# V loaded like q and k and turned on TensorE, and chosen rows fetched by a gathering DMA, in a fused attention and routing kernel

## The chip, the cores and the metric

The kernel runs on one core of one Trainium2 chip, as one launch. The metric is the time of one execution on the device in microseconds. Before the change three runs gave 177.98 us as median, 177.62 the lowest and 179.37 the highest.

## The reference: what is computed

Two stages follow each other. The first is attention in chunks: 4 batches, 8 heads, 768 positions, 64 values per head. Each chunk of 32 queries sees 8 memory rows and the context from 16 positions before the chunk to 8 after it.

```
for c in range(nc):                       # 24 chunks of 32 queries
    k_full = concat(mem_k, k[l_start:r_end])      # 8 memory rows + up to 56 keys
    v_full = concat(mem_v, v[l_start:r_end])
    a = softmax(q_c @ k_full.T / sqrt(64))
    out[c] = a @ v_full
```

The second stage works on the result x (4 x 768 x 512). A gate picks 128 of the 768 rows in each batch, and only these go through two matrix products.

```
scores = x @ w_gate
top_idx = the 128 rows with the highest score
ye = relu(x[top_idx] @ w1) @ w2           # 512 -> 1024 -> 512
out[top_idx] = x[top_idx] + sigmoid(scores[top_idx]) * ye
```

## The kernel before, in words

The unit of work is a *pair*: heads h and h+4 of one batch side by side on the 128 partitions. There are 16 pairs, n = 4b + pr, four to a batch. The queries and keys of a pair fall into 8 groups of 96 queries. All orders are written out by hand: each engine runs its instructions in program order, and a semaphore wait of one holds up everything behind it on that engine.

**Loads.** q and k come through POOL's queue, cast to fp16 on the way, as rows of 8 positions x 64 values (512 fp32, 2 KB) on 96 partitions (`load_qk`, L79). V comes through the queues of SP and ACT uncast (`load_v`, L83), as rows of two keys (128 fp32, 512 B), with keys on partitions: for each group 60 partitions of key pairs and 4 of memory pairs, in each half of the partitions one head. Neighbouring groups share keys, so each group's 120 keys are read again: 60 x 8 rows per head. All loads of a batch are issued together, two batches ahead.

**A pair.** `tr_q` and `tr_k` turn q and k with 16 small transposes each into one PSUM tile `p_t`, of which there is one; ACT copies q out (L219), DVE copies k out in two instructions (L228), POOL adds the memory keys (L235). `cast_v` copies V's pairs to fp16 (L243 on ACT, L245 on DVE). `scores(n, half)` does 16 matmuls with 64 rows and 64 columns of the array (L261) and three exponentials on ACT (L266). `values(n, half)` does 24 matmuls with 64 rows of the array each, accumulating the even and the odd keys (L287); the two heads use the upper and the lower 64 rows. `normalise` divides by the row sums once per pair on DVE (L294, L295).

**The order.** Iteration n of the main loop (L497) runs scores(n+1, 0), tr_k(n+2), values(n, 0), cast_v(n+2), scores(n+1, 1), tr_q(n+3), values(n, 1), normalise(n). In six gaps per iteration (`hook`) a step of the second stage of the batch before is put in: dot products with the gate vector on DVE (`m_dot`), a transpose that spreads the scores over a row (`m_row`, L345), casts of x to fp16 on ACT (`m_x16`, L339), comparisons of all scores on DVE (`m_cmp`, L369), counts by matmul (`m_count`, L379), selection matrices (`m_select`, L398), the gather of the chosen rows by 24 matmuls with these matrices (`m_gather`, L406), index and gate by six matmuls more (`m_aux`, L416), and the two products (`m_ffn1` L431, `m_ffn2` L440). The result times the gate (L443) is added to the output by an indirect DMA (L444). The last batch's second stage follows the loop (L534 on).

Of the kernel before, what the change touches and what calls it, by code (L numbers as in the profile page):

```python
# [26 lines left out]
def kernel(  # L27
# [55 lines left out]
    def load_v(b, p0, n, engines=(nc.sync, nc.scalar)):  # L83


        t = vbufs[b % 2].rearrange("p n g d -> p (n g) d")
        u = NG * p0
        for hh in range(2):
            h = 4 * hh + p0
            lo = 1 if (b, h) == (0, 0) else 0  # L90
            hi = NG * n - 1 if (b, h + n) == (B - 1, H) else NG * n
            o = 64 * hh
            base = (b * H + h) * HD - 16 * D
            engines[hh].dma_start(out=t[o:o + 60, u + lo:u + hi, :],
                                  in_=_dap(v, base + 96 * D * lo, [[2 * D, 60], [96 * D, hi - lo], [1, 128]]))
            if lo:
                engines[hh].dma_start(out=t[o + 8:o + 60, u, :], in_=_dap(v, base + 16 * D, [[2 * D, 52], [1, 128]]))
            if hi < NG * n:
                engines[hh].dma_start(out=t[o:o + 56, u + hi, :],  # L99
                                      in_=_dap(v, base + 96 * D * hi, [[2 * D, 56], [1, 128]]))  # L100
        for hh in range(2):
            for i in range(n):
                nc.sync.dma_start(out=t[64 * hh + 60:64 * hh + 64, u + NG * i:u + NG * (i + 1), :],
                                  in_=_dap(mem_v, (b * H + 4 * hh + p0 + i) * n_mem * D,
                                           [[2 * D, 4], [0, NG], [1, 128]]))
# [481 lines left out]
```

## Time and profile before

| | before |
|---|---|
| median of 3 runs | 177.98 us |
| the profiled execution: device time | 178.1 us |
| its span, first to last instruction | 176.3 us |
| mean granted TensorE clock | 0.873 |
| PE (matmuls) busy | 118.3 us, 67% |
| DVE busy | 88.5 us, 50% |
| ACT busy | 82.8 us, 47% |
| POOL busy | 28.5 us, 16% |
| bytes read from HBM, written | 25.49 MB, 7.34 MB |

Busy times are sums over the span; the stages have different limits, so they are read stage by stage. The 1.8 us between span and device time lie around the first and last instruction. The first pair's iteration starts at 25.0 us, the fifth's (batch 1) at 56.5, the ninth's at 94.3, the thirteenth's at 123.9; the loop ends at 152.0.

### The profile page before, as it was taken

The page shows a single profiled execution, that of the slowest core. Times are in us where ns is not written, and L with a number is a line of the kernel's source. Part 1 is how long each engine was busy: PE and PEld are TensorE (multiplying, and loading weights), DVE is VectorE, ACT ScalarE, POOL GpSimd, SP SyncE. Part 2 cuts the span into 40 slices and gives each one's busy share as a digit, 9 for nine tenths or more (in the row PEclk, how much of TensorE's full clock was granted, in tenths as well). Part 3 has the DMA queues.
Part 4 walks back from the last instruction along what each step waited for, and adds up shares of the span by engine and source line. Part 5 has one row for each costly group of instructions (what it writes and reads, how often), then busy time and mean ns, then how long its engine had stood idle before and what let it go on. Part 6 is the DMA issues. An engine that isn't in the chain of part 4 may idle for free.

```text
span 176.3 us, 5308 instructions
## 1 busy us (share of the span) xinstructions
PE 118.3 (67%) x2280; PEld 95.9 (54%) x2280; DVE 88.5 (50%) x275; ACT 82.8 (47%) x163; POOL 28.5 (16%) x57
## 2 busy tenths in 40 slices
PE   0005379996019999798198875999878687456820
PEld 0005367885018878687165565887656576245700
DVE  2303403650035978854025979733897592775010
ACT  0001399650076879431554796447779046030300
POOL 7805900500000113000003300000500000200030
PEclk9999999999999999999858997569995559965795
DMA  5999999999999898999920465000159000059104
GB/s 127 215 223 205 229 216 226 231 227 218 209 194 269 217 116 156 290 264 181 189 60 5 63 200 161 6 0 4 13 128 279 10 0 4 0 77 294 51 0 59
DMA packets 29211, 24.75 MB, mean 140 GB/s; under 512 B 1423, under 2 KB 24963, under 8 KB 29187
## 3 DMA queue, kind: packets, MB, share of 16 engines
q0 software_dynamic: 9136, 9.47, 34.0%
q1 hardware_dynamic: 12271, 11.01, 24.4%
q10 hardware_dynamic: 7780, 3.93, 9.9%
q8 instruction: 18, 0.29, 0.7%
q14 instruction: 6, 0.05, 0.1%
HBM read 25.49 MB, written 7.34 MB: 186 GB/s over the span
## 4 chain that ended last, share of the span: by engine, by line
DMA 31%; PE 28%; DVE 18%; ACT 7%; issue 7%; ACTq 4%; POOLq 1%; SPq 0%; DVEq 0%
DMA v<-in_v_dram 19%; PE p_x L287 8%; DMA v<-in_mem_v_dram 6%; DVE gr L369 6%; PE p_t L211 5%; DVE junk L332 5%; PE p_m L440 4%; DMA out_dram<-x 4%; PE p_s L261 4%; PE p_m L431 3%; ACTq L99 3%; PE p_m L406 3%; ACT es L266 3%; DMA out_dram<-y,idx 3%; DVE x L295 2%
## 5 line engine op out<-in xcount | busy, mean ns | idle before, releaser
L266 ACT ACTIVATE es<-p_s,maskb 128x256 f16<-128x256 f32 x96 | 38.9, 489 | 26.1 <-PE p_s L261 20.4
L287 PE MATMUL p_x<-vc,es 64*96 64x65 f16 (+1 forms) x768 | 31.8, 235 | 0.7 <-DVE x L295 0.7
L287 PEld LDWEIGHTS <-es 64*96 64x96 f16 (+1 forms) x768 | 25.3, 136 | 5.3 <-issue 0.6
L228 DVE COPY kw<-p_t 128x480 f16<-128x480 f16 x32 | 19.5, 650 | 13.7 <-PE p_t L211 13.7
L261 PE MATMUL p_s<-qT,kw 64*64 64x96 f16 x512 | 23.7, 255 | 0.5 <-ACT es L266 0.5
L444 POOL DMA_INDIRECT out_dram<-y,idx x4 | 6.8, 1700 | 95.1 <-PE p_t L211 54.2
L261 PEld LDWEIGHTS <-kw 64*64 64x64 f16 x512 | 18.5, 143 | 4.6 <-issue 2.2
L211 PE MATMUL p_t<-ident,k 96*64 96x96 f16 x256 | 11.7, 254 | 11.8 <-ACT qT L219 11.8
L243 ACT CAST vc<-v 128x768 f16<-128x768 f32 x16 | 13.8, 861 | 10.8 <-DMA v<-in_mem_v_dram 10.8
L211 PEld LDWEIGHTS <-k 96*64 96x64 f16 x256 | 9.4, 143 | 13.2 <-issue 12.2
L332 DVE SCALAR_TENSOR_TENSOR junk<-x,wgb 128x512 f32<-128x512 f32 (+2 forms) x30 | 16.0, 579 | 0.1
L295 DVE TENSOR_TENSOR x<-p_x,rd 128x768 f32<-128x768 f32 x16 | 15.3, 957 | 0.6
L211 PE MATMUL p_t<-ident,q 96*64 96x96 f16 x256 | 12.3, 263 | 3.8 <-DVE kw L228 3.8
L219 ACT COPY qT<-p_t 128x768 f16<-128x768 f16 x16 | 13.1, 817 | 3.4 <-PE p_t L211 3.4
L294 DVE RECIPROCAL rd<-p_x 128x12 f32<-128x12 f32 x16 | 3.7, 228 | 21.8 <-PE p_x L287 21.8
L369 DVE TENSOR_SCALAR gr<-brow,scr 128x768 f16<-128x768 f32 x24 | 13.3, 614 | 0.1
L211 PEld LDWEIGHTS <-q 96*64 96x64 f16 x256 | 10.1, 149 | 5.3 <-issue 4.2
L245 DVE TENSOR_SCALAR vc<-v,ones 128x128 f16<-128x128 f32 x32 | 7.6, 290 | 10.4 <-DMA v<-in_mem_v_dram 10.0
L339 ACT CAST x<-x 128x1024 f16<-128x1024 f32 (+2 forms) x11 | 12.6, 1148 | 0.0
L431 PEld LDWEIGHTS <-w_sb 128*128 128x128 f16 x128 | 8.7, 108 | 6.4 <-issue 4.4
L379 PEld LDWEIGHTS <-gr 128*128 128x128 f16 x144 | 5.4, 104 | 10.3 <-DVE gr L369 10.0
L431 PE MATMUL p_m<-xeT,w_sb 128*128 128x128 f16 x96 | 7.2, 236 | 5.5 <-ACT hT L433 4.5
(90 smaller groups left out, 115.5 us busy)
## 6 DMA issues: line engine op xcount, KB each, us to landing
out_dram<-x SPq DMA_DIRECT2D x4, 1152.0 KB
v<-in_v_dram SPq DMA_DIRECT2D x3, 960.0 KB
q<-in_q_dram POOLq DMA_DIRECT2D x6, 384.0 KB, 12.3
k<-in_k_dram POOLq DMA_DIRECT2D x6, 384.0 KB, 14.9
w_sb<-in_moe_w_dram POOLq DMA_DIRECT2D x2, 1024.0 KB, 24.2
v<-in_v_dram ACTq DMA_DIRECT2D x2, 960.0 KB
out_dram<-x SPq DMA_DIRECT2D x4, 384.0 KB
v<-in_v_dram ACTq DMA_DIRECT2D x1, 930.0 KB
```

The costliest lines, as they stand in the source:

```text
L211: nc.tensor.transpose(out=p_t[64 * h:64 * h + 64, j, 2:98], in_=src[b][:, pr + 4 * h, 64 * j:64 * j + 64], identity=ident16[0:96, 0:96])
L219: nc.scalar.copy(out=qT, in_=p_t[:, :, 2:98].rearrange("p j t -> p t j"))
L228: nc.vector.tensor_copy(out=kw[:, :, s, 0:60].rearrange("p g (t j) -> p g t j", j=4), in_=_sap(p_t, 100 * s, [[12, NG], [1, 15], [200, 4]]))
L243: nc.scalar.copy(out=vc[:, 1:7, :, 0:64], in_=vt[:, pr, 1:7, :].rearrange("p g (s d) -> p g s d", d=D))
L261: nc.tensor.matmul(out=p_s[o:o + 64, s, 96 * gi:96 * gi + 96], lhsT=kw[o:o + 64, g, s, :], rhs=qf[o:o + 64, 96 * g:96 * g + 96], start=Tru ...
L266: nc.scalar.activation(out=es[:, :, :, 32 * c:32 * c + 32], in_=pv[:, :, :, 32 * c:32 * c + 32], func=AF.Exp, bias=maskb[:, c:c + 1], scal ...
L287: nc.tensor.matmul(out=p_x[r0:r1, h, c0:c0 + 65], lhsT=es[o:o + 64, s, gi, q0:q1], rhs=vc[o:o + 64, GROUPS[half][gi], s, :], start=(s == 0 ...
L295: nc.vector.tensor_tensor(out=xs[b].rearrange("p g (h n d) -> p n h g d", n=NP, d=D)[:, pr], in0=pv[:, :, :, 0:64], in1=rd.to_broadcast([1 ...
L332: nc.vector.scalar_tensor_tensor(out=o, in0=i, scalar=1.0, in1=w, op0=ALU.mult, op1=ALU.mult, accum_out=dst[:, bl:bl + 1])
L339: nc.scalar.copy(out=o, in_=i)
L369: nc.vector.tensor_scalar(out=m.gr[:, bl, :], in0=m.brow, scalar1=m.scr[:, bl:bl + 1], scalar2=None, op0=ALU.is_lt)
L431: nc.tensor.matmul(out=p_h[:, 0, 128 * fi:128 * fi + 128], lhsT=w1_sb[:, dch, f0:f0 + 128], rhs=m.xeT[:, dch, :], start=(dch == 0), stop=( ...
```

## The change

V is loaded exactly like q and k, through POOL's queue, as 2 KB rows cast to fp16. It is turned by 16 transposes into `p_t` (`tr_v`), copied by ACT into groups of 128 keys with 15 + 1 columns (15 of the sequence, one memory row) per eight, and turned back by eight 128 x 128 transposes per pair (`back_v`), so that all 128 keys of a group lie on the partitions. k gets the same column layout. Scores then need 8 matmuls per half (64 rows, 128 columns of the array) in place of 16, values 12 with all 128 rows in place of 24, and each half is normalised by itself. k's copy out of `p_t` becomes one DVE instruction of 1024 elements with unit step, and so is the copy of V's back-transposes. An iteration has eight hooks in place of six, and the second stage's steps are spread over them. For batches 0 to 2 the chosen rows are fetched from the output in HBM by an indirect DMA with 128 indices (`m_fetch`), transposed in fp32 (`m_rows`), and their gate is computed from them (`m_gate1`); the casts of x, the gather by matmul and the two-part gate remain for the last batch only. The gated result is written by ACT in place of DVE. Indirect DMAs name the output only up to the batch in question.

```diff
+    pvv = ctx.enter_context(tc.tile_pool(name="pvv", bufs=1, space=bass.MemoryType.PSUM))
...
-    def load_v(b, p0, n, engines=(nc.sync, nc.scalar)):
...
+    def load(b, src, dst, h0, n, step=1):
         nc.gpsimd.dma_start(out=dst[:, h0:h0 + step * (n - 1) + 1:step, :],
                             in_=_dap(src, (b * H + h0) * HD, [[512, 96], [step * HD, n], [1, 512]]))
...
+    def load_batch(b):
+        for h0 in (0, 4):
+            load(b, k, k16s[b], h0, 4)
+            load(b, v, v16s[b], h0, 4)
+            load(b, q, q16s[b], h0, 4)
...
+    for src, dst in ((mem_k, memk16), (mem_v, memv16)):
+        nc.gpsimd.dma_start(out=dst, in_=_dap(src, 0, [[D, n_mem], [n_mem * D, B * H], [1, D]]))
+    load(0, v, v16s[0], 0, 2, 4)
     for pr in range(1, NP):
-        load_qk(0, k, k16s[0], pr, 2, 4)
-        load_qk(0, q, q16s[0], pr, 2, 4)
+        load(0, k, k16s[0], pr, 2, 4)
+        load(0, q, q16s[0], pr, 2, 4)
+        load(0, v, v16s[0], pr, 2, 4)
...
+    def mem_cols(t, src, n):
+        nc.gpsimd.tensor_copy(out=t.rearrange("p g (j t) -> p g j t", t=16)[:, :, :, 15],
+                              in_=src[:, n:n + 1, :].to_broadcast([128, NG, n_mem]))
     def tr_k(n):
...
-        for s in range(2):
-            nc.vector.tensor_copy(out=kw[:, :, s, 0:60].rearrange("p g (t j) -> p g t j", j=4),
-                                  in_=_sap(p_t, 100 * s, [[12, NG], [1, 15], [200, 4]]))
+        nc.vector.tensor_copy(out=kw.rearrange("p g (j t) -> p g j t", t=16),
+                              in_=_sap(p_t, 0, [[12, NG], [100, 8], [1, 16]]))
+        mem_cols(kw, memkT, n)
+    def tr_v(n):
...
+        transposes(v16s, n)
+        vw = vws[n % SLOTS]
+        nc.scalar.copy(out=vw.rearrange("p g (j t) -> p g j t", t=16),
+                       in_=_sap(p_t, 0, [[12, NG], [100, 8], [1, 16]]))
+        mem_cols(vw, memvT, n)
-    def cast_v(n):
...
+    def back_v(n):
...
+        p_v = pvv.tile([128, NG, 2, D], F16, tag="pv", name="p_v")
+        for g in range(NG):
+            nc.tensor.transpose(out=p_v[:, g, :, :], in_=vws[n % SLOTS][:, g, :], identity=ident16)
+        nc.vector.tensor_copy(out=vcs[n % SLOTS][:, :, :, 0:64], in_=p_v)
...
-            for s in range(2):
-                for h in range(2):
-                    o = 64 * h
-                    nc.tensor.matmul(out=p_s[o:o + 64, s, 96 * gi:96 * gi + 96], lhsT=kw[o:o + 64, g, s, :],
+            for h in range(2):
+                o = 64 * h
+                nc.tensor.matmul(out=p_s[:, h, 96 * gi:96 * gi + 96], lhsT=kw[o:o + 64, g, :],
+                                 rhs=qf[o:o + 64, 96 * g:96 * g + 96], start=True, stop=True)
...
+        p_x = pxx.tile([128, 3, 2, 65], FP, tag="px", name="p_x")
...
+                for h in range(2):
+                    nc.tensor.matmul(out=p_x[r0:r1, i, h, :], lhsT=es[:, h, gi, q0:q1],
+                                     rhs=vc[:, GROUPS[half][gi], h, 0:65], start=True, stop=True)
+        rd = att.tile([128, 3, 2, 1], FP, tag="rd", name="rd")
+        nc.vector.reciprocal(out=rd, in_=p_x[:, :, :, 64:65])
...
+    def m_fetch(b):
...
+        for bl in range(NB):
+            nc.tensor.matmul(out=p_a[:, 0, 0:1], lhsT=m.sel[:, bl, :], rhs=auxs[0][:, bl, 0:1],
+                             start=(bl == 0), stop=(bl == NB - 1))
+        m.idx = mod.tile([128, 1], I32, tag="idx", name="idx")
+        nc.vector.tensor_scalar(out=m.idx, in0=p_a[:, 0, 0:1], scalar1=float(b * S), scalar2=None, op0=ALU.add)
+        m.xe = mod.tile([128, Dm], FP, tag="xe", name="xe")
+        nc.gpsimd.indirect_dma_start(out=m.xe[:, :], out_offset=None, in_=outf[0:(b + 1) * S, :],
+                                     in_offset=bass.IndirectOffsetOnAxis(ap=m.idx[:, :1], axis=0))
+    def m_rows(b):
...
+        for dch in range(4):
+            nc.tensor.transpose(out=p_e[:, 0, 128 * dch:128 * dch + 128], in_=m.xe[:, 128 * dch:128 * dch + 128],
+                                identity=ident)
+        nc.scalar.copy(out=m.xeT.rearrange("p c t -> p (c t)"), in_=p_e[:, 0, :])
+    def m_gate1(b):
...
+        nc.vector.scalar_tensor_tensor(out=junk, in0=m.xe, scalar=1.0, in1=wgb, op0=ALU.mult, op1=ALU.mult,
+                                       accum_out=se)
+        nc.scalar.activation(out=m.gate, in_=se, func=AF.Exp, scale=-1.0)
+        nc.vector.tensor_scalar(out=m.gate, in0=m.gate, scalar1=1.0, scalar2=None, op0=ALU.add)
+        nc.vector.reciprocal(out=m.gate, in_=m.gate)
...
-        nc.vector.tensor_scalar(out=y, in0=p_y[:, 0, :], scalar1=m.gate[:, 0:1], scalar2=None, op0=ALU.mult)
-        nc.gpsimd.indirect_dma_start(out=outf, out_offset=bass.IndirectOffsetOnAxis(ap=m.idx[:, :1], axis=0),
+        nc.scalar.activation(out=y, in_=p_y[:, 0, :], func=AF.Copy, scale=m.gate[:, 0:1])
+        nc.gpsimd.indirect_dma_start(out=outf[0:(b + 1) * S, :], out_offset=bass.IndirectOffsetOnAxis(ap=m.idx[:, :1], axis=0),
...
+        st = {i: [lambda i=i: m_dot(b, (i,))] for i in range(NB)}
+        st[0].insert(0, lambda: m_alloc(b))
+        st[6] = [lambda: m_row(b, 0, 4)]
+        st[8] = [lambda: m_row(b, 4, 6)]
+        for i in range(NB):
+            st[9 + i] = [lambda i=i: m_cmp(b, (i,))]
+        st[14].append(lambda: m_count(b, range(0, 3)))
+        st[15] = [lambda: m_count(b, range(3, 6)), lambda: m_mask(b)]
+        st[17] = [lambda: m_select(b)]
+        st[19] = [lambda: m_fetch(b)]
+        st[24] = [lambda: m_rows(b), lambda: m_gate1(b)]
+        st[26] = [lambda: m_ffn1(b, 0)]
+        st[28] = [lambda: m_ffn1(b, 1)]
+        st[30] = [lambda: m_ffn2(b)]
...
+    mem_rows(memk16, memkT)
     tr_k(0)
-    mem_k(0)
     tr_q(0)
+    mem_rows(memv16, memvT)
+    tr_v(0)
+    scores(0, 0)
     tr_k(1)
+    back_v(0)
+    scores(0, 1)
     tr_q(1)
+    tr_v(1)
     tr_q(2)
     alloc_batch(1)
+    load_batch(1)
...
         scores(n + 1, 0)
         hook(0)
         tr_k(n + 2)
         hook(1)
         values(n, 0)
         hook(2)
+        tr_v(n + 2)
+        hook(3)
         scores(n + 1, 1)
+        hook(4)
+        back_v(n + 1)
+        hook(5)
+        values(n, 1)
+        hook(6)
         tr_q(n + 3)
+        hook(7)
         if pr == 2 and b + 2 < B:
             alloc_batch(b + 2)
+            load_batch(b + 2)
```

## Rows read from the trace of the kernel before

**Rows 1.** The page's span in 40 equal slices: mean busy share of the DMA engines, tenths.
```profile
DMA  5999999999999898999920465000159000059104
```

**Rows 2.** The chain that ended last: start us, length us, what.
```profile
24.67 24.56 DMA v<-in_v_dram
...
79.74 5.86 ACTq L99
...
153.10 4.46 DMA out_dram<-y,idx
```

**Rows 3.** Timeline of PE, first half: start us, us, operation, count, idle before.
```profile
13.89 1.02 PE L170 MATMUL p_mk<-ident,memk 8*64 8x8 f16 x32 [13.89 <-DMA memk<-in_mem_k_dram]
...
24.99 0.85 PE L261 MATMUL p_s<-qT,kw 64*64 64x96 f16 x16 [0.53 <-ACT es L266]
...
34.64 0.85 PE L211 MATMUL p_t<-ident,q 96*64 96x96 f16 x16
35.42 1.13 PE L287 MATMUL p_x<-vc,es 64*96 64x65 f16 x24
36.48 0.85 PE L261 MATMUL p_s<-qT,kw 64*64 64x96 f16 x16
37.26 0.85 PE L211 MATMUL p_t<-ident,k 96*64 96x96 f16 x16
...
52.07 0.85 PE L211 MATMUL p_t<-ident,k 96*64 96x96 f16 x16 [9.50 <-ACT qT L219]
...
61.77 1.11 PE L345 MATMUL p_m<-ident,scr 128*128 128x128 f32 x4
...
87.38 1.86 PE L431 MATMUL p_m<-xeT,w_sb 128*128 128x128 f16 x16 [4.46 <-ACT hT L433]
```

**Rows 4.** DMA queues in two stretches of 4 us, 48:52 and 84:88: packets, MB, share.
```profile
q0 software_dynamic: 750, 0.74, 110.9%
...
q10 hardware_dynamic: 1326, 0.68, 101.2%
```

**Rows 5.** Windows of L211 (transposes): PE busy (count), PEld busy (count), granted clock, DMA, GB/s.
```profile
52.00:56.00 4.00, 1.70 (x32) 1.32 (x31) 1.00 1.10 247
...
88.00:92.00 4.00, 0.85 (x16) 0.66 (x16) 0.50 0.35 69
```

**Rows 6.** Timeline of PE, second half.
```profile
102.76 0.53 PE L211 MATMUL p_t<-ident,q 96*64 96x96 f16 x16
103.22 0.75 PE L287 MATMUL p_x<-vc,es 64*96 64x65 f16 x24
103.90 0.53 PE L261 MATMUL p_s<-qT,kw 64*64 64x96 f16 x16
...
113.24 2.74 PE L406 MATMUL p_m<-sel,x 128*128 128x128 f16 x24
...
117.73 1.12 PE L431 MATMUL p_m<-xeT,w_sb 128*128 128x128 f16 x16
```

**Rows 7.** Groups by line and form: count, busy us, mean ns, idle before.
```profile
L228 DVE COPY kw<-p_t 128x480 f16<-128x480 f16 x32 | 19.5, 650 | 13.7 <-PE p_t L211 13.7
L295 DVE TENSOR_TENSOR x<-p_x,rd 128x768 f32<-128x768 f32 x16 | 15.3, 957 | 0.6
L369 DVE TENSOR_SCALAR gr<-brow,scr 128x768 f16<-128x768 f32 x24 | 13.3, 614 | 0.1
L219 ACT COPY qT<-p_t 128x768 f16<-128x768 f16 x16 | 13.1, 817 | 3.4 <-PE p_t L211 3.4
L245 DVE TENSOR_SCALAR vc<-v,ones 128x128 f16<-128x128 f32 x32 | 7.6, 290 | 10.4 <-DMA v<-in_mem_v_dram 10.0 <-issue 0.4
L294 DVE RECIPROCAL rd<-p_x 128x12 f32<-128x12 f32 x16 | 3.7, 228 | 21.8 <-PE p_x L287 21.8
L443 DVE TENSOR_SCALAR y<-p_m,gate 128x512 f32<-128x512 f32 x3 | 2.3, 751 | 3.3 <-PE p_m L440 3.3
```

**Rows 8.** Waits: engine, line, waited for: us in total, times, longest us.
```profile
PE p_m L379 <- DVE gr L369: 6.0, 10, 1.4
```

More of the change, by code (lines that the diff above doesn't have):

```diff
@@ L67 @@
     ctx.enter_context(tc.manual_schedule())
-    q16s, k16s = {}, {}
-    vbufs = [cst.tile([128, NP, NG, 128], FP, tag=f"v32_{i}", name=f"v32_{i}") for i in range(2)]
+    q16s, k16s, v16s = {}, {}, {}
     def alloc_batch(b):
@@ L77, in alloc_batch @@
         k16s[b] = ld.tile([96, H, 512], F16, tag="k16", name=f"k16_{b}")
-    def load_qk(b, src, dst, h0, n, step=1):
+        v16s[b] = ld.tile([96, H, 512], F16, tag="v16", name=f"v16_{b}")
+    def load(b, src, dst, h0, n, step=1):
         nc.gpsimd.dma_start(out=dst[:, h0:h0 + step * (n - 1) + 1:step, :],
                             in_=_dap(src, (b * H + h0) * HD, [[512, 96], [step * HD, n], [1, 512]]))
-    def load_v(b, p0, n, engines=(nc.sync, nc.scalar)):
[L86 to L105, printed above, removed]
+    def load_batch(b):
[3 more added lines that the diff above has]
+            load(b, q, q16s[b], h0, 4)
     alloc_batch(0)
-    load_qk(0, k, k16s[0], 0, 2, 4)
-    load_qk(0, q, q16s[0], 0, 2, 4)
+    memk16 = cst.tile([n_mem, B * H, D], F16, tag="memk16")
+    memv16 = cst.tile([n_mem, B * H, D], F16, tag="memv16")
+    load(0, k, k16s[0], 0, 2, 4)
+    load(0, q, q16s[0], 0, 2, 4)
     ident16 = cst.tile([128, 128], F16, tag="ident16")
@@ L169, in mem_keys @@
             for hh in range(2):
-                nc.tensor.transpose(out=p_mk[64 * hh:64 * hh + 64, pr, :], in_=memk16[:, b * H + 4 * hh + i, :],
+                nc.tensor.transpose(out=p_mk[64 * hh:64 * hh + 64, pr, :], in_=src[:, b * H + 4 * hh + i, :],
                                     identity=ident16[0:n_mem, 0:n_mem])
-        nc.vector.tensor_copy(out=memkT, in_=p_mk.rearrange("p n (j s) -> p n s j", s=2))
+        nc.vector.tensor_copy(out=dst, in_=p_mk)
     ident = cst.tile([128, 128], FP, tag="ident")
@@ L498 @@
         b, pr = divmod(n, NP)
-        steps = moe_steps(b - 1) if b >= 1 else [[] for _ in range(24)]
+        steps = moe_steps(b - 1) if b >= 1 else {}
         def hook(i):
-            for f in steps[6 * pr + i]:
+            for f in steps.get(8 * pr + i, ()):
                 f()
@@ L509 @@
         tr_k(n + 2)
-        mem_k(n + 2)
         hook(1)
         values(n, 0)
-        cast_v(n + 2)
         hook(2)
+        tr_v(n + 2)
+        hook(3)
         scores(n + 1, 1)
-        hook(3)
+        hook(4)
[3 more added lines that the diff above has]
+        hook(6)
         tr_q(n + 3)
-        hook(4)
-        values(n, 1)
-        normalise(n)
-        hook(5)
+        hook(7)
         if pr == 2 and b + 2 < B:
             alloc_batch(b + 2)
-            for h0 in (0, 4):
-                load_qk(b + 2, q, q16s[b + 2], h0, 4)
-                load_qk(b + 2, k, k16s[b + 2], h0, 4)
-            load_v(b + 2, 0, NP)
+            load_batch(b + 2)
         if n == NPR - 2:
```

116 lines of the change are left out of this document (30 added, 86 removed).

## The prediction

> **What bounds the kernel now.** I read the page's 40 slices first: the DMA engines are nearly full from 0.5 us to about 60 and again from 66 to 90 [rows 1], so the first half may be waiting for data. Then the chain of waits: two of its pieces are transfers or queues of V, 24.56 us for batch 1's rows and 5.86 us in which ACT's queue is held at the issue of batch 3's V (L99) [rows 2]. What they cost is read from PE's timeline, not from their length: PE stands 9.50 us before 52.07 and 4.46 us before 87.38 [rows 3], 14.0 us together. Apart from these two gaps PE sets the pace of the first half alone: from start to start 16 transposes take 0.78 us, a half of values 1.06, a half of scores 0.78 [rows 3], and a pair has two of each: 5.24 us with no gap. In the second half PE is not alone: a pair needs 2 x (0.46 + 0.68) us plus two scores of about 0.46, 3.2 us [rows 6], but batch 2 takes 29.6 us (94.3 to 123.9); DVE's comparisons alone keep PE's counts waiting 6.0 us in all [rows 8].
>
> The two sets of durations are TensorE's two clock levels. At 52 to 56 us the granted clock reads 1.00, yet 32 transposes are 1.70 us busy, exactly the 0.85 per 16 of 88 to 92 us, where it reads 0.50 [rows 5]; at 102.76 us 16 take 0.53 [rows 6]. So durations decide, and the whole first half runs at 1.2 GHz, with PE without a gap from 52 to 76 us. In this trace 2.4 GHz comes only behind the gather's or the FFN's 128 x 128 matmuls: the gather starts at 113.24 and runs at 0.11 us a matmul, the FFN matmuls at 117.73 take 1.12 us where the same 16 took 1.86 at 87.38 [rows 3, 6].
>
> **The change part by part**, against the profiled execution's 178.1 us (span 176.3 plus 1.8 outside). That is 0.1 from the median of 177.98, so no correction is needed. A measurement of this kernel can tell about 1% from no change.
>
> *V's transfer.* Before, V is 60 x 8 rows of 512 B per head, 15,360 packets; where they run almost alone, 1326 of them fill 101.2% of 16 engines for 4 us, 49 ns each; a 2 KB row of POOL's queue costs 95 ns by the same count (750 at 110.9%) [rows 4]. V becomes 32 x 96 = 3072 such rows: 47 us of all 16 engines (15,360 x 49 / 16) become 18. The two gaps go: **-14.0**. What is late next: batch 1's 2304 rows of k, v and q need 12.3 us at the rate of 48 to 52 us (750 in 4 us [rows 4]). POOL issues them behind the memory copy for the second V, which waits for ACT, at about 22 us. They land near 36, just when the second iteration ends and wants q. If that cover fails, every us late is a us lost, to some 4 us.
>
> *The head.* PE's first work waits for the memory keys until 13.89 [rows 3], behind q, k and V of three queues. With V's packets gone from the two other queues they land earlier, but not before the 384 rows of k and q in front (2 us): between 6 us and no gain; I take 9, -5. The way to the first iteration (24.99 [rows 3], 11.1 us later) gets longer by the second memory transpose (1.02), two turns of V through p_t (0.78 and a copy of up to 1.09 each, below) and back_v (0.9), partly beside each other: +3.5. **-1.5** (from -6 to +3).
>
> *PE per pair.* Added: tr_v, 0.78, and back_v, eight 128 x 128 passes at the gather's 2.67 / 24 = 0.11 [rows 6], 0.9. Scores: four slots of two heads in place of eight, each from 0.10 (0.78 / 8) to 0.11: 0.5 with the change of shape, so 2 x 0.28 less. Values: 12 slots then, 12 now, since the two heads ran in pairs in one half of the rows each: nothing, at both levels. A new wait: tr_k follows tr_q after one half of scores (0.5 us) and needs p_t back from ACT's copy (0.82, L219 [rows 7]); everything on PE stands behind it: 0.4. Sum 1.11 + 0.4 = 1.5 in ten pairs that run at the low level and are bound by PE (n = 0 to 7, 10, half of 11 and half of 14): **+15.0**. At the high level the added 0.6 lies beside DVE and ACT in n = 8, 9, 12, 13 and costs nothing; if these got faster it would cost 2.4 in all.
>
> *DVE.* Per pair 2 x 650 + 2 x 290 + 228 + 957 = 3.07 us before [rows 7]. Normalising by halves adds the fixed part of two more instructions each, about 0.2 (the 228 ns for 12 elements is nearly all that): 1.6. No row copies 1024 fp16 from PSUM with unit step. At L228's 1.35 ns an element (it steps 200 elements) a copy takes 1.39 us, at L369's 0.80 (unit step, from SBUF) 0.82. I take 0.82, because the unit step is what changed: 2 x 0.82 + 1.6 = 3.24. The gated write leaves DVE (0.75, L443 [rows 7]), and the small gate steps too. **-1.5** over the loop; at 1.39 instead +5 there. The Trainium skill (VectorE: DVE Perf Modes, "Why PSUM operands drop a tier") says a 16-bit copy from PSUM with unit step goes at up to two elements a cycle. By its table a copy would be about 0.66 us, an estimate, and the sum about 2 us lower; no row here shows it from PSUM.
>
> *ACT.* 1024 elements for V's copy, at most 0.817 x 1024 / 768 = 1.09 us in place of a cast that lay beside PE; hidden by PE's 6.7 us per pair. The casts of x and their removal are off the path too.
>
> *The gather.* Three times 2.67 us of PE go (-8.0), and four fp32 transposes come, 1.1 us by L345 [rows 3] (+3.3). The index matmuls cost what L416's did. The fetch needs its index, POOL's issue and the landing: an indirect DMA of as many rows took 4.46 [rows 2], which I take for the gather, between 2 and 7. PE has scores, back_v, values, tr_q and scores before m_rows, 3.7 us: it waits about 1.3 each time (+4). **-0.7**. Behind it on PE stand tr_k and all that follows.
>
> *Clock.* The gather was one of the two things that 2.4 GHz came behind. Without it the first FFN half and some attention of n = 7, 11 and 15 fall to 1.2 GHz: 0.74 us per FFN half [rows 3, 6], about 2 with attention, in two of three batches: **+4** (0 to +10).
>
> *Spreading.* Comparisons stand one per hook with attention between them and the counts: of the 6.0 us [rows 8] I give back **-4**. *End.* The last batch's dot products no longer wait for L443: **-0.7**. The rest of the tail, 24 us behind the loop, is unchanged.
>
> Sum: -14.0 - 1.5 + 15.0 - 1.5 - 0.7 + 4 - 4 - 0.7 = -3.4, so **174.7 us**. The change pays for the DMA gaps with almost as much TensorE work, and its own range is 170 to 180 by the bounds above.
>
> **The rivals.**
>
> *The clock rises in the attention loop.* back_v is 0.9 us of 128 x 128 passes per pair, the kind behind which 2.4 GHz came, and scores use all columns. For it: every rise stands behind such passes. [...] A pair would then be bound by p_t's three turns and ACT, about 4.5 instead of 6.7: 8 x 2.2 less some 5 for batch 1's rows, which do not come earlier, gives -13, and n = 10, 11 and 14 another -4: **157 to 160 us**. The Trainium skill (TensorE: Matmul & The Clock Gate, "The HAM clock gate") has it that sustained matmul activity by itself releases the throttle, by which this rival would be the forecast. The gapless low-clock stretch from 52 to 76 us [rows 5] contradicts it.
>
> *The clock stays low until the FFN and falls before the next batch gains from it.* Place: n = 8, 9, 12, 13, which now run at the high level under DVE. Price: each goes from about 5.2 to 6.7, +6, and the FFNs of n = 11 and 15 another +4: **184 us**, slower. It decides as soon as 2.4 GHz is not there when the batch's first iteration starts. For it: the gather is gone from every batch of the loop. Against: after the FFN of batch 0 the level held beyond 103.9 us [rows 6].
>
> *DVE copies at the old rate.* k's copy of 1.39 outlasts the 1.06 of values before tr_v: 0.4 in ten pairs, and 5 in the DVE-bound ones: +9, **183 us**. For it: L228 is the only such copy measured [rows 7].
>
> *V is not the cause.* If POOL's queue moved a batch no sooner, the gaps would stay, 174.7 + 14.0 = 189; the chain's naming of V [rows 2] speaks against it.
>
> **How the numbers follow.** Forecast 0.46, clock up 0.24, clock low 0.17, slow copies 0.10, V not the cause 0.03. The likeliest case's time is 174.7, and its own range is 170 to 180; faster by over 1% is below 176.2, which two thirds of it are (0.31), with 0.09 within 1% and 0.06 above. With the rivals: faster 0.31 + 0.24 = 0.55; same 0.09 + 0.04 of the slow cases' near ends = 0.13; slower 0.32. The range from 158 to 184 takes in most of the clock rivals and leaves out about 0.2.
>
> **What would show it.** PE's gaps before 52 and 87 us gone; POOL's queue alone on the load; a low-clock pair of 6.5 to 7.0 us in batch 0; scores 0.5 per half, values 1.06, back_v 0.9; DVE's 1024-element copies near 0.8; a wait of m_rows for the fetch of 1 to 2 us. The forecast is wrong if 16 transposes take 0.53 before 60 us (clock up), if a batch 0 pair stays at or below 5.3, or if batch 1's q is late by more than 4 us.

## The result, and the profile after

The changed kernel takes **172.81 us** (median of 4, 171.36 to 174.28), the kernel before on the same chip 177.80 (176.66 to 179.37): ratio **0.966, 95% interval 0.957 to 0.975**. A later set of the unchanged new kernel (e12 below) gave 173.75 and 0.970, 0.964 to 0.977. The forecast was 174.7. Ratios leave out executions more than 1.5% above the fastest of the same kernel; the profiles of e2, e3, e4, e8, e10 and e11 come from such executions, and from these only single steps and clock levels are read. The profiled execution took 171.51 us, its span 169.8.

The page's slices, granted clock and DMA, tenths:

```profile
PEclk9999999999999995558999955589996556965696
DMA  4999269999999960199995002007900010790022
```

The DMA row now has holes at 17 to 21 us and 64 to 72 us; before it was full up to about 60 and again from 66 to 90 [rows 1]. POOL's DMA queue over the whole span (packets, MB, share of 16 engines):

```profile
q0 software_dynamic: 13136, 13.44, 48.7%
```

V's loads are now on POOL's q0 with those of q and k; q10 with V's 512 B rows [rows 4] no longer appears. PE's timeline (start us, us, operation, count, idle before and its releaser): the first wait for q and one whole low-clock pair behind it, the rise of the clock, and the other waits for data in the loop:

```profile
36.69 0.85 PE L194 MATMUL p_t<-ident,q 96*64 96x96 f16 x15 [2.31 <-DMA q<-in_q_dram]
37.47 0.50 PE L247 MATMUL p_s<-qT,kw 64*128 64x96 f16 x8
38.43 0.85 PE L194 MATMUL p_t<-ident,k 96*64 96x96 f16 x16 [0.45 <-ACT qT L202]
39.21 1.14 PE L268 MATMUL p_x<-vc,es 128*96 128x65 f16 x12
40.28 0.85 PE L194 MATMUL p_t<-ident,v 96*64 96x96 f16 x16
41.06 0.50 PE L247 MATMUL p_s<-qT,kw 64*128 64x96 f16 x8
41.49 1.03 PE L232 MATMUL p_v<-ident,vw 128*128 128x128 f16 x8
42.33 1.10 PE L268 MATMUL p_x<-vc,es 128*96 128x65 f16 x12
43.36 0.85 PE L194 MATMUL p_t<-ident,q 96*64 96x96 f16 x16
44.14 0.50 PE L247 MATMUL p_s<-qT,kw 64*128 64x96 f16 x8
...
50.02 0.74 PE L194 MATMUL p_t<-ident,q 96*64 96x96 f16 x16
50.70 0.34 PE L247 MATMUL p_s<-qT,kw 64*128 64x96 f16 x8
51.65 0.53 PE L194 MATMUL p_t<-ident,k 96*64 96x96 f16 x16 [0.61 <-ACT qT L202]
...
63.26 0.53 PE L194 MATMUL p_t<-ident,q 96*64 96x96 f16 x15 [1.40 <-DMA q<-in_q_dram]
...
65.16 0.85 PE L194 MATMUL p_t<-ident,k 96*64 96x96 f16 x16
...
73.60 1.09 PE L395 MATMUL p_m<-ident,xe 128*128 128x128 f32 x4 [1.76 <-DMA xe<-out_dram,idx]
...
106.00 1.08 PE L395 MATMUL p_m<-ident,xe 128*128 128x128 f32 x4 [1.48 <-DMA xe<-out_dram,idx]
...
108.86 1.89 PE L441 MATMUL p_m<-xeT,w_sb 128*128 128x128 f16 x16
...
137.19 1.09 PE L395 MATMUL p_m<-ident,xe 128*128 128x128 f32 x4 [1.86 <-DVE junk L310]
```

Read it in three steps. V's waits of 9.50 and 4.46 us [rows 3] have no successor of their size: the longest is 2.31 us, for batch 1's q. From the scores at 37.47 to those at 44.14 a pair takes 6.67 us, 0.45 of it a wait for qT; before it was 5.24. And at 51.65 sixteen transposes take 0.53 us where at 43.36 they took 0.85 (busy; 0.78 from start to start): TensorE went to 2.4 GHz near 50.5 us, just as batch 1's first iteration starts and ahead of any second-stage work on TensorE, which the kernel before never did. At 65.16 us sixteen take 0.85 again.

Iterations start at 21.55 (24.99 before [rows 3]), the first of batch 1 at 50.70 (56.53), of batch 2 at 83.64 (94.30), the loop ends at 145.76 (152.03). By stage, against the forecast's terms:

| stage | forecast | measured, us |
|---|---|---|
| to the first iteration | -1.5 | -3.4 |
| batch 0 | -9.5 + 4 x 1.5 = -3.5 | 31.5 to 29.2: -2.4 |
| batch 1 | -4.5 + 6.0 - 1.6 = -0.1 | 37.8 to 32.9: -4.8 |
| batches 2 and 3 | +4 + 3.0 - 1.5 - 3.1 = +2.4 | 57.7 to 62.1: +4.4 |
| behind the loop | -0.7 | 24.3 to 24.0: -0.3 |
| sum | -3.4 | -6.5 |

(1.6 and 3.1 are one and two thirds of the 4.7 us forecast for the gather and the spreading; +4 is the clock, 3.0 two low-clock pairs, -1.5 DVE.)

### The profile page after: what moved, and what is told of

It reads as the page before. It is cut to its first block, busy times and chain, and to the rows that moved or that the text cites. A ratio compares the mean times of both kernels' runs of the same rounds, so it can differ in the third digit from the quotient of the medians.

```text
span 169.8 us, 4653 instructions
## 1 busy us (share of the span) xinstructions
PE 124.0 (73%) x1996; PEld 100.8 (59%) x1996; DVE 86.0 (51%) x266; ACT 81.5 (48%) x158; POOL 52.5 (31%) x87
## 4 chain that ended last, share of the span: by engine, by line
PE 32%; DMA 18%; ACT 14%; DVE 14%; issue 12%; POOL 4%; POOLq 1%; DVEq 0%; ACTq 0%
PE p_t L194 9%; DMA q<-in_q_dram 7%; PE p_x L268 6%; DVE gr L347 6%; ACT es L252 5%; DMA out_dram<-y,idx 4%; PE p_m L441 4%; DMA xe<-out_dram,idx 4%; DVE kw L214 4%; ACT qT L202 3%; PE p_m L450 3%; PE p_v L232 3%; DMA memk<-in_mem_k_dram 2%; DVE x L272 2%; PE p_s L247 2%
## 5 line engine op out<-in xcount | busy, mean ns | idle before, releaser
L268 PE MATMUL p_x<-vc,es 128*32 128x65 f16 (+1 forms) x384 | 30.1, 232 | 0.0
L268 PEld LDWEIGHTS <-es 128*32 128x32 f16 (+1 forms) x384 | 24.9, 136 | 3.3
L223 ACT COPY vw<-p_t 128x1024 f16<-128x1024 f16 x16 | 16.2, 1012 | 17.8 <-DVE x L272 6.6
L214 DVE COPY kw<-p_t 128x1024 f16<-128x1024 f16 x16 | 11.1, 691 | 26.9 <-PE p_t L194 24.5
L202 ACT COPY qT<-p_t 128x768 f16<-128x768 f16 x16 | 12.8, 801 | 12.4 <-PE p_t L194 12.3
L233 DVE COPY vc<-p_v 128x1024 f16<-128x1024 f16 x16 | 11.0, 686 | 15.3 <-PE p_v L232 15.3
L272 DVE TENSOR_TENSOR x<-p_x,rd 128x384 f32<-128x384 f32 x32 | 17.8, 557 | 1.1
L247 PE MATMUL p_s<-qT,kw 64*128 64x96 f16 x256 | 13.9, 243 | 0.4 <-POOL kw L206 0.4
L194 PE MATMUL p_t<-ident,v 96*64 96x96 f16 x256 | 11.4, 249 | 2.8 <-ACT qT L202 1.6
L232 PE MATMUL p_v<-ident,vw 128*128 128x128 f16 x128 | 13.2, 265 | 0.0
L194 PEld LDWEIGHTS <-v 96*64 96x64 f16 x256 | 9.6, 139 | 3.9 <-issue 2.9
```

The costliest lines, as they stand in the source:

```text
L194: nc.tensor.transpose(out=p_t[64 * h:64 * h + 64, j, 2:98], in_=src[b][:, pr + 4 * h, 64 * j:64 * j + 64], identity=ident16[0:96, 0:96])
L202: nc.scalar.copy(out=qT, in_=p_t[:, :, 2:98].rearrange("p j t -> p t j"))
L214: nc.vector.tensor_copy(out=kw.rearrange("p g (j t) -> p g j t", t=16), in_=_sap(p_t, 0, [[12, NG], [100, 8], [1, 16]]))
L223: nc.scalar.copy(out=vw.rearrange("p g (j t) -> p g j t", t=16), in_=_sap(p_t, 0, [[12, NG], [100, 8], [1, 16]]))
L232: nc.tensor.transpose(out=p_v[:, g, :, :], in_=vws[n % SLOTS][:, g, :], identity=ident16)
L247: nc.tensor.matmul(out=p_s[:, h, 96 * gi:96 * gi + 96], lhsT=kw[o:o + 64, g, :], rhs=qf[o:o + 64, 96 * g:96 * g + 96], start=True, stop=True)
```

## The experiments

Three questions: did V's transfer hold the first half up; is the gain V's or the gathering DMA's; and what does the clock do.

**e1: the kernel before, without V's loads.**

```diff
-        vc, vt = vcs[n % SLOTS], vbufs[b % 2]
+        vc, vt = vcs[n % SLOTS], vbufs[0]
...
-    load_v(1, 0, NP)
...
-            load_v(b + 2, 0, NP)
```

> The kernel before, without V's loads for batches 1 to 3 (batch 0's V is used in their place; nothing else is changed). Theory (V's transfer held the first half up, its price is PE's two gaps of 9.5 and 4.5 us): the time falls by about 14 us from 177.8 to 164, PE's gaps before 52 and 87 us are gone, and a pair of batch 0 and 1 stays near 5.2 us. Rival 1 (the gaps stand for another transfer, k's or q's on POOL's queue): 177, gaps still there. Rival 2 (without the gaps the clock rises earlier or falls earlier): more than 3 us away from 164, and the 16 transposes take 0.53 us where they now take 0.78, or the other way round.

161.44 us, ratio 0.904 (0.896 to 0.911). PE's timeline of e1 where the 9.5 us gap was:

```profile
47.67 0.85 PE L211 MATMUL p_t<-ident,k 96*64 96x96 f16 x16
48.45 1.13 PE L287 MATMUL p_x<-vc,es 64*96 64x65 f16 x24
49.51 0.85 PE L261 MATMUL p_s<-qT,kw 64*64 64x96 f16 x16
```

No row has a wait, and pairs stay at 5.24. Batch 0 takes 22.0 us for 31.5, exactly the gap less; batch 1 30.6 for 37.8, which is the second gap and 2.7 more; batches 2 and 3 together +0.8. Most of the 2.7 is TensorE's clock: before, the FFN behind the second gap ran at the low level, in e1 at the high one. The FFN of batch 0 in the kernel before, around the half at 87.38 that [rows 3] shows, and then in e1:

```profile
80.72 1.07 PE L431 MATMUL p_m<-xeT,w_sb 128*128 128x128 f16 x16
...
91.02 3.35 PE L440 MATMUL p_m<-w_sb,hT 128*128 128x512 f16 x8
```
```profile
73.54 1.07 PE L431 MATMUL p_m<-xeT,w_sb 128*128 128x128 f16 x16
...
75.68 1.90 PE L440 MATMUL p_m<-w_sb,hT 128*128 128x512 f16 x8
```

Its second half (1.86 at 87.38) and L440 together are 5.21 us before and 2.97 in e1, 2.2 less. V's loads cost 17 us, of which the two gaps show 14. Rival 1 falls. The change keeps 5 of these 17; the longer pairs (6.67 for 5.24 us) are the largest part of what it pays back.

**e2: the changed kernel with the gather back in place of the fetch.**

```diff
-        st[19] = [lambda: m_fetch(b)]
-        st[24] = [lambda: m_rows(b), lambda: m_gate1(b)]
+        st[22] = [lambda: m_gather(b)]
+        st[24] = [lambda: m_aux(b)]
...
-        st[8] = [lambda: m_row(b, 4, 6)]
+        st[7] = [lambda: m_x16(b, 2, 4)]
+        st[8] = [lambda: m_row(b, 4, 6), lambda: m_gate(b)]
```

> The changed kernel with the rows of batches 0 to 2 chosen as before: six casts of x to fp16, 24 matmuls of 128 x 128 for the gather, gate and index by the auxiliary matmuls, in place of the gathering DMA, the four fp32 transposes and the gate of the chosen rows. V's new way stays. Theory (the fetch is about neutral, the gain is V's): 170 to 175, within 2 us of 172.8. Rival 1 (the gain of 5 us is the gather's removal): 178. Rival 2 (the clock's fall in batches 2 and 3 comes from the missing gather): under 170, with the high level (16 transposes in 0.53 us) held through n = 10 and 11, where it falls at 98 us in the changed kernel.

175.28 us (169.88 to 175.58); too spread for a ratio. It is not a clean undoing. DVE's and ACT's timelines of e2:

```profile
61.75 0.17 DVE L334 TENSOR_SCALAR gt<-gt 128x6 f32<-128x6 f32 x1 [3.81 <-ACT gt L333]
...
62.47 0.69 DVE L214 COPY kw<-p_t 128x1024 f16<-128x1024 f16 x1
```
```profile
59.18 1.05 ACT L316 CAST x<-x 128x1024 f16<-128x1024 f32 x1
...
61.46 0.25 ACT L333 ACTIVATE gt<-scr 128x6 f32<-128x6 f32 x1
```

I had put the gate's exponential behind two casts on ACT, DVE waits 3.81 us for it, and k's copy, behind it on DVE, keeps PE waiting 2.47, 2.27 and 2.12 us in the three batches. These 6.9 us come from my placement. The time stays below rival 1's 178 even with them, which speaks against the gather's removal as the source of the 5 us; how fetch and gather compare e2 does not show, and that stays open.

**e3: loads earlier.**

```diff
     tr_k(1)
+    alloc_batch(1)
+    load_batch(1)
     back_v(0)
...
-        if pr == 2 and b + 2 < B:
+        if pr == 1 and b + 2 < B:
```

> The changed kernel with batch 1's six loads issued on POOL right behind the second pair's memory copy (from about 16.7 us instead of 21.0), where POOL is idle for 4.0 us, and the loads of batches 2 and 3 at the end of the second instead of the third pair. Theory (batch 1's q is late by the issue alone): PE's waits for q of 2.31 us before 36.69 and 1.40 us before 63.26 go, 172.8 - 3.7 = 169 us. Rival (the rows land no sooner, because the queue is full of batch 0's and the weights' rows, or a later wait takes their place): 171.5 to 173.

170.84 us, 0.951 (0.941 to 0.961) against the unchanged 0.970 (0.964 to 0.977): both waits for q are gone and some 3 us are gained by the ratios, of the 3.7 expected. But batch 3's rows now stood ahead of the first fetch on POOL's queue. POOL's and PE's timelines of e3:

```profile
61.97 0.67 POOL L80 DMA_DIRECT2D q<-in_q_dram  x1
...
67.24 1.08 POOL L388 DMA_INDIRECT xe<-out_dram,idx  x1 [0.46 <-issue]
```
```profile
74.50 1.09 PE L395 MATMUL p_m<-ident,xe 128*128 128x128 f32 x4 [5.38 <-DMA xe<-out_dram,idx]
```

The fetch took 7.1 us from issue to landing there (median 3.3 in the changed kernel) and PE stood 5.38 us for it.

**e4: q's turn ahead of the second half of values.**

```diff
-        values(n, 1)
-        hook(6)
         tr_q(n + 3)
+        hook(6)
+        values(n, 1)
```

> The changed kernel with q's turn put ahead of the second half of values, so that ACT's copy of qT (0.80 us) lies beside values (1.06 us) and the next half of scores instead of beside scores alone. Theory (PE stands 0.45 us a pair at the low level and 0.6 to 0.73 at the high level for that copy, the term of 0.4 in the forecast): 0.45 x 8 + 0.65 x 4 = 6 us less, 167. Rival 1 (in batches 2 and 3 DVE or ACT paces the loop, so only the low-level pairs gain): 169. Rival 2 (q's turn then waits for ACT's copy of V out of the same bank, 1.01 us, which is as long as the scores and back turn between them): no gain, 172.8.

172.18 us, 0.963 (0.953 to 0.974): no difference from 0.970 that can be told. The step itself did what it should: the waits for qT are gone and a low-clock pair is 6.31 for 6.67 us. But PE's wait for batch 1's q grew from 2.31 to 3.05 us, and in the profiled execution the clock stayed low until the FFN near 79 us. Neither theory (167) nor rival 1 (169) holds. Rival 2's time does, but not its reason: of the 0.45 us only about 0.1 came back as a wait for ACT's copy of V.

**e5: no turns of V.**

```diff
+        if n >= NP:
+            return
         transposes(v16s, n)
...
+        if n >= NP:
+            return
         p_v = pvv.tile([128, NG, 2, D], F16, tag="pv", name="p_v")
```

> The changed kernel without V's two turns (16 transposes, ACT's copy, eight 128 x 128 passes, DVE's copy) for pairs 4 to 15: batch 0's V stands in for the others'. V is still loaded. Theory (V's turns are what the change pays with, 0.78 + 0.82 us a pair where PE paces the loop): pairs at the low level fall from 6.67 to about 5.1 us; with some seven such pairs behind pair 2, 172.8 - 11 = 162, about what the kernel before gave without V's loads (161.4). Rival 1 (the turns lie beside ACT and DVE, and the change's price is elsewhere): over 169. Rival 2 (the rise of the clock at 50.5 us came from the 128 x 128 passes of back_v and goes with them): no rise before the first gather or FFN, and pairs 4 to 7 all at the low level; the time is then some 2 us above the theory's.

168.27 us, 0.944 (0.937 to 0.951). Turning V is paid on the path, but not with 11 us: some 5. PE's timeline of e5:

```profile
44.15 0.85 PE L194 MATMUL p_t<-ident,k 96*64 96x96 f16 x16 [0.46 <-ACT qT L202]
...
46.94 1.14 PE L272 MATMUL p_x<-vc,es 128*96 128x65 f16 x12 [0.45 <-DVE x L276]
...
49.75 0.85 PE L194 MATMUL p_t<-ident,k 96*64 96x96 f16 x16 [0.46 <-ACT qT L202]
```

With the turns gone, values follow scores at once and wait 0.45 us here, up to 1.10 later, for DVE to empty the one bank of p_x; a pair is 5.60, not 5.1. And the low level lasted: after a short high stretch at 27 to 31 us, sixteen transposes take 0.78 us from start to start from 38 to 78 us and again from 88 to 109. For pairs 4 to 7 that is what rival 2 expected of the clock, but its time (some 2 us above 162) is not met either. The high stretch at 27 us stands in a part of the program that is the changed kernel's own, whose two profiles are low there.

**e6: back_v twice.**

```diff
-        for g in range(NG):
+        for g in [*range(NG), *range(NG)]:
```

> The changed kernel with back_v's eight 128 x 128 transposes made twice into the same bank (the values are the same). Theory (PE paces the loop at the low level): +0.85 us for each low-level pair, nine or ten of them, and nothing at the high level: 172.8 + 8 = 181. Rival (the clock's rise in the attention loop hangs on these passes, and twice as many bring it earlier and hold it): 16 transposes at 0.47 us before 45 us and through most of batch 1, pairs near 5.3 us, 166 to 171.

169.47 us, 0.956 (0.949 to 0.962). More work on TensorE made the kernel faster than its own unchanged version: by 2 to 4 us, as one compares ratios (0.966 and 0.970 unchanged) or medians (172.81 and 173.75). The longest of its four executions, 170.34, is shorter than the shortest of ten unchanged ones, 171.36. The theory falls; the rival's time and levels are met. PE's timeline of e6 at the turn:

```profile
41.96 1.89 PE L232 MATMUL p_v<-ident,vw 128*128 128x128 f16 x16
43.64 0.93 PE L268 MATMUL p_x<-vc,es 128*96 128x65 f16 x12
44.50 0.53 PE L194 MATMUL p_t<-ident,q 96*64 96x96 f16 x16
```

The sixteen passes run at 1.2 GHz (1.68 us to the next start), the values behind them are in between (0.93), and the next transposes run at 2.4 GHz, until 64 us. Whether the doubled passes brought this rise is taken up behind e12.

**e7: the fetched rows two steps later.**

```diff
-        st[24] = [lambda: m_rows(b), lambda: m_gate1(b)]
-        st[26] = [lambda: m_ffn1(b, 0)]
-        st[28] = [lambda: m_ffn1(b, 1)]
+        st[26] = [lambda: m_rows(b), lambda: m_gate1(b)]
+        st[28] = [lambda: m_ffn1(b, 0)]
+        st[29] = [lambda: m_ffn1(b, 1)]
```

> The changed kernel with the fp32 transposes of the fetched rows and their gate two steps later (behind the first half of values instead of behind scores), the first FFN halves two and one steps later. Theory (PE's waits of 1.76, 1.48 and 1.86 us are the fetch's landing): they go, 172.8 - 5.1 = 168. Rival 1 (the later FFN brings the high clock later and the waits move to the gated write or the next batch's store): 171 to 174. Rival 2 (the wait is DVE's gate, which stands behind the fetch, not the fetch): the waits move with it, 172.8.

171.55 us, 0.969 (0.963 to 0.976): no gain that can be told. No wait for the fetch is left, but the wait for batch 2's q grew to 3.59 us, since the loop reached it sooner: in the profiled execution, with 169.70 the shortest of the four, the clock rose at 43.5 us. PE's timeline of e7:

```profile
43.52 0.34 PE L247 MATMUL p_s<-qT,kw 64*128 64x96 f16 x8
```

Up to there the program is that of the changed kernel, with one back_v. The time is rival 1's.

**e8: e3 (with batch 3's loads where they were), e4 and e7 together.**

```diff
     tr_k(1)
+    alloc_batch(1)
+    load_batch(1)
...
-        if pr == 2 and b + 2 < B:
+        if pr == (1 if b == 0 else 2) and b + 2 < B:
...
-        values(n, 1)
-        hook(6)
         tr_q(n + 3)
+        hook(6)
+        values(n, 1)
...
+        st[26] = [lambda: m_rows(b), lambda: m_gate1(b)]
```

> The changed kernel with batch 1's and batch 2's loads early (batch 3's at the old place, since its rows stood in front of the first fetch, 5.38 us, when they were moved too), q's turn ahead of the second half of values, and the fetched rows turned two steps later. Theory (each removes a wait of PE): -3.7 for q's rows, -0.4 x 8 for p_t, -4 for the fetch: 162 to 164. Rival (the clock's level decides, and shorter waits only let DVE and ACT pace batches 2 and 3): 168 to 171.

168.86 us (166.17 to 171.37; too spread for a ratio). The waits for q and for the fetch are gone and a pair is 6.31; its profiled execution stayed at the low level until 76 us. The time is the rival's.

**e9: k's turn twice, the control for e6.**

```diff
         transposes(k16s, n)
+        transposes(k16s, n)
```

> The changed kernel with k's 16 transposes of 96 rows made twice (0.78 us more on TensorE per pair at the low level, as much as the second back_v of the run before it; the values are the same). Theory (the clock's rise in the attention loop hangs on passes over all 128 rows, of which these are none): no earlier rise than in the changed kernel, and low-level pairs 0.8 us longer: 178 to 181. Rival (any more work on TensorE brings the rise, so the doubled back_v was nothing special): high level from about 45 us through most of batch 1 and 169 to 171, as with back_v twice.

178.85 us, 1.000 (0.996 to 1.005): 5 us slower than unchanged, for 0.64 us more of TensorE in a low-clock pair (7.31 for 6.67), while e6, which is faster, added 0.85 (1.68 for 0.82). The rival falls, and the theory's time holds. Its clock does not quite: the profiled execution goes high from 20 to 22 us, where the changed kernel's two profiles are low, and from 53 to 66, about where the changed kernel's first one did.

**e10: e3 (batch 3 as before), e7 and e6 together.**

```diff
+        for g in [*range(NG), *range(NG)]:
...
+        st[26] = [lambda: m_rows(b), lambda: m_gate1(b)]
...
+        if pr == (1 if b == 0 else 2) and b + 2 < B:
```

> The changed kernel with early loads for batches 1 and 2, the fetched rows turned two steps later, and back_v made twice; q's turn at its old place. Theory (with back_v twice the high level comes near 44 us and stays through batch 1, and the waits for q and for the fetch are gone): 169.5 - 1.6 - 2.3 - 2 = 164. Rival 1 (the second back_v costs what it brings once the loop has no waits): 167 to 169, as the combination without it. Rival 2 (without the wait for q PE stays at the low level until the FFN): 172.

**166.26 us, 0.928 (0.921 to 0.935)**, the best of the kernels that do all the work, between the theory's 164 and rival 1's 167. PE's timeline of e10:

```profile
39.04 0.34 PE L247 MATMUL p_s<-qT,kw 64*128 64x96 f16 x8
...
44.16 0.34 PE L247 MATMUL p_s<-qT,kw 64*128 64x96 f16 x8
...
58.51 0.53 PE L194 MATMUL p_t<-ident,q 96*64 96x96 f16 x15 [2.85 <-DMA q<-in_q_dram]
```

High level from 28 to 59 us, pairs of 5.1 us (39.04 to 44.16); what is late next is again q, now batch 2's.

**e11: e10 and the swap of e4.**

```diff
-        values(n, 1)
-        hook(6)
         tr_q(n + 3)
+        hook(6)
+        values(n, 1)
```

> The same with q's turn ahead of the second half of values. Theory (the swap is what kept the high level away in its two runs, because q's turn then follows back_v at once and no passes over 128 rows stand in the rest of the pair): low level until the FFN of batch 0 near 80 us, 168.9 + 0.85 x 9 = 176. Rival (the level follows the number of 128-row passes, whatever their place): high level from 45 us on, 164.

168.25 us, 0.940 (0.933 to 0.946), between the theory's 176 and the rival's 164. Windows of the transposes (PE busy and count, PEld busy and count, granted clock, DMA share, GB/s) in e8, and then in e11, which differs by the doubled back_v alone:

```profile
30.00:50.00 20.00, 8.26 (x160) 6.57 (x160) 1.00 1.21 206
```
```profile
30.00:50.00 20.00, 6.37 (x192) 5.51 (x192) 1.00 1.19 218
```

16 take 0.83 us in e8 and 0.53 in e11, both under a granted clock of 1.00 (the first stretch's column is no guide, as in [rows 5]). My theory, that the swap keeps the high level away, is wrong: with back_v twice it comes at 27 to 28 us, swap (e11) or not (e10). But the median is only 0.6 us below e8's 168.86, which is no difference that can be told: on top of e8's edits the second back_v gained nothing clear. What is late in e11's profiled execution, its longest, is batch 2's q, by PE's timeline:

```profile
58.65 0.85 PE L194 MATMUL p_t<-ident,q 96*64 96x96 f16 x15 [5.80 <-DMA q<-in_q_dram]
```

**e12: the changed kernel again.**

> The changed kernel, unchanged, on the chip of the runs beside it: how far the time of its executions goes with the time at which the clock rises in the attention loop. Theory (the rise is not tied to one point of the program): executions spread over 171 to 175 us, those with the early rise at the lower end. Rival (the rise always comes at 50.5 us): all within 171 to 172.5.

173.75 us (171.94 to 174.74). The profiled execution took 173.77 us. Windows of the transposes, first in the changed kernel's first profile and then in e12:

```profile
52.00:62.00 10.00, 2.54 (x74) 1.94 (x68) 1.00 1.10 258
```
```profile
52.00:62.00 10.00, 3.53 (x67) 2.65 (x64) 1.00 1.10 263
```

0.55 us per 16 against 0.84: the same program, and in e12 the rise did not come until the FFN, near 79 us. Batch 1 takes 35.0 us there for 32.9, and the span is 2.2 us longer: this is what the early rise was worth between these two executions. The theory holds for them. Across executions the mean granted clock does not sort the times (171.94 at 0.790, but 174.74 at 0.803), so what else moves them stays open.

**Where the rise came in every profile.** From the rows of transposes and scores in PE's timeline, in the loop up to 66 us. "None" means that the first high rows come with batch 0's FFN, at 77 to 80 us.

| profile | back_v | at the high level, us |
|---|---|---|
| changed kernel | once | 50.7 to 64 |
| e12, the same program | once | none |
| e7, the same up to 65 us | once | 43.5 to 60 |
| e2 | once | 57 to 61 |
| e3 | once | 42 to 48 |
| e4, e8 (swap) | once | none |
| e5 | once, for batch 0 alone | 27.5 to 31 |
| e9 (k's turn twice) | once | 20 to 22, 53 to 66 |
| e6 | twice | 44.5 to 64 |
| e10 | twice | 19.5 to 21, 28 to 59 |
| e11 (swap) | twice | 17 to 20, 27 to 53 |

With back_v twice the level is high by 44.5 us in all three profiles and stays so for 16 us and more. With one set only e7 did as well; of the eight others three did not rise at all, and the same program rose at 43.5, at 50.7 or not. So that the second set brings the rise is likely, but not shown: each profile is one execution. What is shown is its effect on time, in e6 against the unchanged kernel and against e9. In five profiles (changed kernel, e6, e7, e10, e11) the first low rows come within 1.5 us behind PE's wait for batch 2's q, of 1.40 to 5.80 us; that the wait ends the high level was not tested.

## Why the prediction was right, point by point

The direction and the main mechanism held: V's gaps went, and the added work on TensorE took most of the gain back. Several sizes did not hold, and that 172.81 lies so near 174.7 is in part luck. Against the forecast's terms in the table by stage (the execution of 171.51 us) the head gave 1.9 us and batch 1 4.7 us more than expected, while batch 0 took 1.1 and batches 2 and 3 2.0 more. One of the forecast's own signs of being wrong also came: 16 transposes at 0.53 us before 60 us, at 51.65 in the profiled execution.

- **V's gaps, -14.0.** Right: both gone in the changed kernel, and e1 shows V's loads as their cause. What the sum put at nothing is that the FFN behind the second gap had run at the low level: 2.2 us in e1. What was late next was named, but with no price in the sum: q cost 2.31 us in batch 1, and 1.40 in batch 2, which I had not seen.
- **The head, -1.5.** Mis-sized: -3.4. Memory keys landed at 7.87, I took 9; the longer way from there is 13.7 us for 11.1, +2.6 for +3.5.
- **PE per pair, 6.7.** Right: 6.67. back_v is 0.82 (0.9), the wait for qT 0.45 (0.4), scores 0.43 to 0.44 (0.5). **Ten pairs** of it, +15.0, was too much: batch 0 paid +4.8 without q's wait and the gap (22.0 to 26.8), not 6.0. e5, which takes the turns out, returns about 5 us only: a low-clock pair falls to 5.60, with waits of 0.45 us and more for DVE and ACT, and in its profile the low level lasts longer.
- **DVE.** Copies and halves of the normalisation, in the groups by line of the changed kernel (line, operation, shapes, count, busy us, mean ns, idle before):

```profile
L272 DVE TENSOR_TENSOR x<-p_x,rd 128x384 f32<-128x384 f32 x32 | 17.8, 557 | 1.1
...
L214 DVE COPY kw<-p_t 128x1024 f16<-128x1024 f16 x16 | 11.1, 691 | 26.9 <-PE p_t L194 24.5 <-PE p_m L370 1.5 <-ACT es L252 0.8
L233 DVE COPY vc<-p_v 128x1024 f16<-128x1024 f16 x16 | 11.0, 686 | 15.3 <-PE p_v L232 15.3
L271 DVE RECIPROCAL rd<-p_x 128x6 f32<-128x6 f32 x32 | 6.1, 190 | 5.8 <-PE p_x L268 5.8
```

  1024 elements take 691 and 686 ns, where L228 took 650 for 480 [rows 7]; I took 0.82. The Trainium skill (VectorE: DVE Perf Modes, "Why PSUM operands drop a tier") was nearer with the estimate of 0.66 worked out from its table, and this trace agrees with it to 5%. The normalisation is 2 x (557 + 190) = 1.49 us, I took 1.6.
- **The gather and the spreading, -0.7 and -4.** Not separated. Waits for the fetch were 1.76, 1.48 and 1.86 where I took 1.3 (the profile names DVE for the third, but that fetch is issued at 133.81 and takes 3.2 to 3.5 us, so it lands just then), and waits of counts fell less than forecast, from 6.0 [rows 8] to 4.1 (the changed kernel's waits: total us, times, longest):

```profile
PE p_m L357 <- DVE gr L347: 4.1, 6, 0.9
```

  The second stage's share of batch 1 fell by 4.0 us, where the forecast has 1.6: before, 37.8 less the gap of 4.46 and four pairs of 5.24 leaves 12.3; in e12, whose attention is at the low level nearly throughout, 35.0 less four pairs of 6.67 leaves 8.3. But 1.6 of the 4.0 is again the FFN of batch 0: 1.07, 1.86 and 3.35 before make 6.28 us, and in PE's timeline of e12 it takes 4.64:

```profile
78.17 1.70 PE L441 MATMUL p_m<-xeT,w_sb 128*128 128x128 f16 x16
...
80.56 1.05 PE L441 MATMUL p_m<-xeT,w_sb 128*128 128x128 f16 x16
...
83.07 1.89 PE L450 MATMUL p_m<-w_sb,hT 128*128 128x512 f16 x8 [0.47 <-ACT hT L443]
```

  Of the 2.4 left, a part is that the 0.45 us wait for qT is covered where second-stage work stands between q's turn and k's. The rest, fetch against gather among it, was not separated (e2).
- **Clock, +4.** The mechanism shows, the size is not measured by itself. In batches 2 and 3 the first FFN half took 1.89 us (108.86 and 139.10) for 1.12 and 1.07 before, near the 0.74 us each of the forecast. The +4.4 of both batches is the sum of all terms, of which +2.4 was forecast. Rows at the low level run there from 109.4 to 117.7 and from 131.1 to about 146 us before, and from 98 to 112 and from 130.7 to about 142 after: 23 and 25 us together, so the low level came earlier rather than lasting longer.
- **First rival, the clock rising in the attention loop.** Half true: it did rise at 50.5 us in the profiled execution and was worth 2.2 us, not 13, because it fell again at 64, behind the wait for batch 2's q. In e12 it did not rise. The rival's pair of 4.5 us at the high level is not reached either: e10, high from 28 to 59 us, takes 5.1.
- **Second rival** (low until the FFN): e12 shows that stage, and the FFN still brought the high level back before batch 2. **Slow DVE copies** and **V not the cause** are excluded by 691 ns and by e1.

The Trainium skill (TensorE: Matmul & The Clock Gate, "The HAM clock gate") holds that sustained matmul work releases the throttle. The traces here bear that out only in part: in e12 PE works at the low level from 8 to 76 us with no wait over 2.2 us, and e8 without one over 0.6 between 21 and 76, so work alone did not do it. The stretch of the kernel before from 52 to 76 us, which the prediction sets against the rule, is not quite gapless: one wait of 1.17 us stands in it, behind 20 us without one.

```profile
72.48 0.32 PE L379 MATMUL p_m<-onec,gr 128*128 128x1 f16 x6 [1.17 <-DVE gr L369]
```

Why one execution of the same program rises at 43.5 us, another at 50.5 and a third not at all was not found.

## What to carry to other kernels

A transfer that holds PE up is worth its gaps, and a little more where the work behind a gap ran at the lower clock level (2.2 us here): remove the transfer alone first and read the ceiling (161.4 here), then ask how much of it the replacement work pays back. Where the clock's level is open, price the loop at both levels, and test whether added passes over all 128 rows pay for themselves: here a useless second set was worth 2 to 4 us alone, and nothing that can be told on top of e8's edits. One profile does not tell when the clock rises; look at several executions before explaining a time with it. Taking one wait away moves the loop to the next (q, then the fetch, then q again), so edits that gain nothing alone belong in one kernel.

## What the hardware showed unexpectedly

- Added TensorE work went both ways: from the unchanged kernel's ratio of 0.970 (173.75 us) eight more 128 x 128 transposes a pair led to 0.956 (169.47), sixteen more of 96 rows to 1.000 (178.85).
- The same program had 16 transposes at 0.55 and at 0.84 us in the same stretch of two executions, and the level rose at 43.5 us in a third (e7, the same program up to 65 us).
- A gathering DMA of 128 rows behind six loads of one queue landed after 7.1 us, with that queue empty after 3.3.
